# Attention and a gated MLP on one core: padding v, pairing the gate's left tokens, and moving the softmax reciprocals

## The chip, the cores and the metric

The kernel runs on one core of a Trainium2 chip. The core has five engines that work in parallel, each through its own queue in order: TensorE (PE in the profile, its weight loads PEld), VectorE (DVE), ScalarE (ACT), GpSimd (POOL) and SyncE (SP), which issues most DMAs. TensorE writes its results to PSUM, in banks of 512 fp32 numbers per partition. The metric is device time in microseconds; the profile is one further execution with its own time.

## The reference

For 8 batches and 12 heads of 448 tokens and 64 features:

```python
def _attn_ref(q, k, v, g_q, g_k):
    q_n, k_n = rmsnorm(q, g_q), rmsnorm(k, g_k)
    scores = matmul(q_n, k_n.T) / sqrt(64)
    attn = exp(scores - max(scores)); attn = attn / (sum(attn) + 1e-09)
    return matmul(attn, v)

def _moe_ref(x, w_in, g_ln, w_sg, b_sg, w_out):      # x: 448 x 768 per batch
    h = gelu(x @ w_in); u, v = h[..., :512], h[..., 512:]
    v_n = layernorm(v) * g_ln
    v_s = einsum('ts,bsd->btd', w_sg, v_n) + b_sg    # mixes tokens: the gate
    return x + (u * v_s) @ w_out
```

The attention result, heads side by side, is the MLP's x. Everything is in float32.

## The kernel before

**Numbers.** A factor in float32 is split into a high and a low float16 part, and a product is three matmuls: high x high, high x low, low x high. So most loops have three parts.

**Tokens.** 448 tokens are three and a half tiles of 128. The kernel holds them as seven chunks of 64 (`C7` = 7, `CM` = 3, `C4` = 4). Work goes by *pairs*: pair i is two heads, 48 pairs in all, six to a batch. Two pairs form a unit u, and their seven tiles of 128 query rows are run through together: tiles 0 to 2 belong to the first pair, tile 3 (`CM`) half to each, tiles 4 to 6 to the second.

**Scores** (L375 to L404). For each tile, matmuls of height 64 (one head in the upper 64 rows of the array, one in the lower) fill a PSUM tile of two banks; there are two such tiles (`NS` = 2). VectorE takes the row maxima (L392), ScalarE the exponentials with their sums (L394) and the copy to float16 (L397), VectorE the low part (L398), and a transposing DMA puts both into `at_all` (L403). After L398 the PSUM tile is free again.

**Reciprocals and row** (`recips`, L406 to L427). GpSimd adds 1e-9 to the sums (L413), VectorE inverts (L414), GpSimd makes high and low halves (L415, L416). Sixteen small matmuls spread the reciprocals along a row for each head (L423), and ScalarE copies it out of PSUM (L426). Row and pv use the same PSUM bank (`NV` = 1).

**pv** (L431 to L456). For each chunk and part, one matmul per head into the lower or upper 64 partitions of the result. Chunks 0 to 2 and 4 to 6 are full, 128 rows by 64 columns; chunk 3 has head 0 in the upper 64 partitions and head 1 in the lower, so its matmuls are quarters of the array, 64 x 64. Then VectorE multiplies by the row (L450), and high and low parts are made (L453, L454). v itself is loaded three pairs at a time (L286), squared for its scale (L353) and split (`vsplit`: L369 on ScalarE, L370 on VectorE). `vh` and `vl` have two buffers each.

**MLP** (`moe`, L477 to L655), one generator per batch: the half x @ w_in that becomes v (L499 to L521; the left 64 tokens first, as a half-width matmul pair at L513, then three tiles at L510), GELU, layer norm, the half that becomes u (L568), the gate (L589 to L609), and the output with the residual (L621 to L651). In the gate each of four blocks f of 128 features takes nine matmuls over the full token tiles and three over the 64 left tokens, which for f = 0, 1 lie in the upper 64 partitions and for f = 2, 3 in the lower. Then VectorE scales (L603), GpSimd multiplies by u (L604), ScalarE rounds (L605), GpSimd makes low parts (L607, L608). `gt` has two buffers; these products share three PSUM banks (`NM`).

**Order.** The work of one turn i is dealt out at L725 to L758: the score generator takes 8 or 6 steps, pv of the pair before `SV` = 4, the MLP of the batch before up to 11 from the third batch on (7 or 8 earlier), the weights 3. A generator's step ends at its next `yield`; the steps are dealt evenly over the turn. A batch's MLP has 46 or 50 steps, so at 11 a turn it fills a little over four of six turns. This order gives each instruction a priority (the MLP's is set 200 back); when the program is built, each engine's queue is ordered by these priorities among what a timeline model holds to be ready. On the chip each queue then runs strictly in that order.

Of the kernel before, what the change touches and what calls it, by code (L numbers as in the profile page):

```python
# [8 lines left out]
F32 = mybir.dt.float32  # L9
F32R = mybir.dt.float32r  # L10
F16 = mybir.dt.float16
BF16 = mybir.dt.bfloat16
I32 = mybir.dt.int32
AF = mybir.ActivationFunctionType
ALU = mybir.AluOpType
# [16 lines left out]

VC, UC = (3,), (0, 1)

SC, SV = 7, 4

NS, NV, NM = 2, 1, 3
NQK, NVR, RAWB = 2, 2, 3
NAT, NAH, NQT, NVH, HLB, GV = 3, 3, 2, 2, 3, 3
NOT, NX = 2, 12  # L40
# [6 lines left out]
def kernel(  # L47
# [16 lines left out]
    P = 128  # L64
# [217 lines left out]
        U[u] = dict(qk=qk)  # L282

    VR = {}

    def load_v(i):  # L286

        if i >= NI:  # L290
            return
        b, g = divmod(i, NP)
        vr = ld.tile([P, GV, C7, D], F32, name="vr", bufs=NVR)
        vp = vr.rearrange("p g c d -> p g (c d)")
        src = v[b, 2 * g:2 * (g + GV)].rearrange("(g h) (p c) d -> h p g (c d)", h=2, c=C7)
        for h, half, s0, c0, n in ((0, lo, 0, 0, C4), (0, hi, 0, C4, CM), (1, lo, C4, C4, CM), (1, hi, CM, 0, C4)):
            nc.sync.dma_start(out=vp[half, :, s0 * D:(s0 + n) * D], in_=src[h][:, :, c0 * D:(c0 + n) * D])
        for j in range(GV):
            VR[i + j] = vr[:, j].rearrange("p c d -> p (c d)")

# [42 lines left out]
    def vsquares(i):  # L343

        if i >= NI:
            return
        b, g = divmod(i, NP)
        if g == 0:
            VS["part", b] = sml.tile([P, NP // GV], F32, name="vpart", bufs=2)
        n = GV * C7 * D  # L350
        sk = prep.tile([P, n], BF16, name="sqv", tag="t4", bufs=HLB)
        x = VR[i]
        A.activation(out=sk, in_=bass.AP(tensor=x.tensor, offset=x.offset, ap=[list(x.ap[0]), [1, n]]), func=AF.Square,  # L353
                     accum_out=VS["part", b][:, g // GV:g // GV + 1])
# [8 lines left out]
    def vsplit(i):  # L363
        r = R.setdefault(i, {})
        sc = VS[i // NP]["sc"]
        vh, vl = (att.tile([P, C7, D], F16, name="v" + c, bufs=NVH) for c in "hl")
        vr = VR.pop(i)
        vf = vh.rearrange("p c d -> p (c d)")
        A.activation(out=vf, in_=vr, func=AF.Copy, scale=sc)  # L369
        V.scalar_tensor_tensor(out=vl.rearrange("p c d -> p (c d)"), in0=vr, scalar=sc, in1=vf, op0=ALU.mult, op1=ALU.subtract)  # L370
        r.update(vh=vh, vl=vl)

    at_all = att.tile([P, 2 * C7, NAT * S], F16, name="at", bufs=1)

    def scores(u):  # L375


        qt = U[u]["qt"]
        sums = sml.tile([P, C7, 2], F32, name="sums", bufs=2)
        U[u]["sums"] = sums  # L380
        for t in range(C7):
            ps = ps_s.tile([P, 2, 512], F32, name="s")

            rows = [(slice(0, P), t // C4)] if t != CM else [(lo, 0), (hi, 1)]
            for m, (qx, kx) in enumerate(((0, 2), (1, 2), (0, 3))):
                for h in range(2):
                    hs = slice(h * HP, (h + 1) * HP)
                    for r_, j in rows:
                        mm(out=ps[r_, h, 0:S], lhsT=qt[hs, qx, t * P + r_.start:t * P + r_.stop],  # L389
                           rhs=qt[hs, kx, j * S:(j + 1) * S], start=(m == 0), stop=(m == 2))  # L390
            nm = sml.tile([P, 2], F32, name="nm", bufs=6)
            V.tensor_reduce(out=nm, in_=ps[:, :, 0:S], axis=AX.X, op=ALU.max, negate=True)  # L392
            for h in range(2):
                A.activation(out=ps[:, h, 0:S], in_=ps[:, h, 0:S], func=AF.Exp, bias=nm[:, h:h + 1], accum_out=sums[:, t, h:h + 1])  # L394
            yield
            ahl = att.tile([P, 2, 2, S], F16, name="ahl", bufs=NAH)
            A.activation(out=ahl[:, 0], in_=ps[:, :, 0:S], func=AF.Copy)  # L397
            V.tensor_tensor(out=ahl[:, 1], in0=ps[:, :, 0:S], in1=ahl[:, 0], op=ALU.subtract)  # L398
            src = ahl.rearrange("p x h n -> p (x h n)")
            o = (NG * u * S + t * P) % (NAT * S)  # L400
            for r_ in ([slice(0, P)] if o + P <= NAT * S else [lo, hi]):
                o1 = (o + r_.start) % (NAT * S)
                nc.sync.dma_start_transpose(out=at_all[:, :, o1:o1 + r_.stop - r_.start], in_=src[r_])  # L403
            yield  # L404

    def recips(i):  # L406

        u, j = divmod(i, NG)
        cs = slice(0, C4) if j == 0 else slice(CM, C7)
        sums = U[u]["sums"][:, cs].rearrange("p t h -> p (t h)")  # L410
        x, y = (sml.tile([P, 2 * C4], F32, name=f"r{c}", bufs=2) for c in "xy")
        rh, rl = (sml.tile([P, 2 * C4], F16, name=f"r{c}", bufs=2) for c in "hl")
        G.tensor_scalar(out=x, in0=sums, scalar1=1e-9, scalar2=None, op0=ALU.add)  # L413
        V.reciprocal(out=y, in_=x)  # L414
        G.tensor_copy(out=rh, in_=y)  # L415
        G.tensor_tensor(out=rl, in0=y, in1=rh, op=ALU.subtract)  # L416
        ps = ps_v.tile([P, 512], F32, name="row", tag="pv")[:, 0:S]
        for n, t in enumerate(range(cs.start, cs.stop)):
            ks, o = (slice(0, P), t * P - j * S) if t != CM else ((lo, SM), (hi, 0))[j]
            for rx in (rh, rl):  # L420
                for h in range(2):
                    w = ks.stop - ks.start
                    mm(out=ps[h * HP:(h + 1) * HP, o:o + w], lhsT=rx[ks, 2 * n + h:2 * n + h + 1].broadcast_to([w, HP]),  # L423
                       rhs=ident_h[ks, ks], start=(n == 0 and rx is rh), stop=(n == CM and rx is rl), skip_group_check=True)
        row = att.tile([P, S], F32, name="row", bufs=1)
        A.activation(out=row, in_=ps, func=AF.Copy)  # L426
        return row  # L427

    XT = {}

    def pv(i):  # L431
        r = R[i]
        vh, vl = r["vh"], r["vl"]
        o = i % NAT * S

        steps = [[(slice(0, P), c + h * C4) if c < CM else (slice(h * HP, (h + 1) * HP), CM) for h in range(2)]
                 for c in range(C4)]
        blocks = [(vx, n, hx) for vx, n in ((vh, 0), (vl, 0), (vh, C7)) for hx in steps]

        blocks = blocks[CM::C4] + [x for n, x in enumerate(blocks) if n % C4 != CM]  # L440
        row = recips(i)
        yield
        ps = ps_v.tile([P, 512], F32, name="pv")[:, 0:S]
        for k_, (vx, n, hx) in enumerate(blocks):
            for h, (ks, c) in enumerate(hx):
                mm(out=ps[h * HP:(h + 1) * HP], lhsT=vx[ks, c], rhs=at_all[ks, n + c, o:o + S],  # L446
                   start=(k_ == 0), stop=(k_ == len(blocks) - 1), skip_group_check=True)
            if k_ in (4, 8):
                yield
        V.tensor_tensor(out=ps, in0=ps, in1=row, op=ALU.mult)  # L450
        xh = xp.tile([P, S], F16, name="xh")
        xl = xp.tile([P, S], F16, name="xl")
# [1 line left out]
        V.tensor_tensor(out=xl, in0=ps, in1=xh, op=ALU.subtract)  # L454
        XT[i] = (xh, xl)
        del R[i]  # L456


    def cluster(acts, done):
# [17 lines left out]
    def moe(b, early=False):  # L477
# [21 lines left out]
        for st, (t, g) in enumerate(steps):  # L499
# [17 lines left out]
                psv[t] = vg[:, tiles[t][1]]  # L517
            if early and t == 1 and g == NP - 1:
                cluster([gelu_v(i) for i in range(2)], done)
            if st % 2 == 1:  # L520
                yield  # L521
        cluster([gelu_v(t) for t in order if not early or t == CM or t > 1], done)
        for t in range(CK):
# [54 lines left out]
                 for f in range(FT)], done)  # L578
        yield
        gh = mlp.tile([P, FT, S], F32R, name="gh", tag="vggh")  # L580
        gl = []
        vh, vl = V2["vh"], V2["vl"]
        half = slice(b % 2 * HP, (b % 2 + 1) * HP)
        if b % 2 == 0:
# [1 line left out]
        else:  # L586
            gth, gtl, _ = GT[b - 1]
        bb = W["bb"]
        for f in range(FT):  # L589
            ps = ps_m.tile([P, 512], F32, name="ms_", tag="mm")  # L590
            n = 0
            for t in range(CK):
                p0, p1, o = 0, P, t * DH + f * P
                if t == CM:
                    p0 = f // 2 * HP
                    p1, o = p0 + HP, t * DH + f % 2 * P
                for vx, wx in ((vh, ws_h), (vh, ws_l), (vl, ws_h)):
                    mm(out=ps[:, 0:S], lhsT=vx[p0:p1, o:o + P], rhs=wx[p0:p1, t], start=(n == 0), stop=(n == 11))
                    n += 1
                if t == 1:  # L600
                    yield
            gt = mlp.tile([P, S], F32, name="gt", tag="gt", bufs=NOT)
            V.scalar_tensor_tensor(out=gt, in0=ps[:, 0:S], scalar=W["gw"][:, f:f + 1], in1=bb, op0=ALU.mult, op1=ALU.add)  # L603
            G.tensor_tensor(out=gt, in0=gt, in1=u[f], op=ALU.mult)  # L604
            A.activation(out=gh[:, f], in_=gt, func=AF.Copy)  # L605
            gl.append(mlp.tile([P, S], F32R, name="gl", tag="ug", bufs=5))
            G.tensor_tensor(out=gl[f], in0=gt, in1=gh[:, f].bitcast(F32), op=ALU.subtract)  # L607
            G.tensor_tensor(out=gtl[:, f, half], in0=gt[:, SM:S], in1=gh[:, f, SM:S].bitcast(F32), op=ALU.subtract)  # L608
            yield  # L609
        idn = VS[b]["idn"]  # L610
        om = [out[x].rearrange("(p c) e -> c p e", c=C7) for x in (b - b % 2, b)]
# [180 lines left out]
```

## Time and profile before

| | |
|---|---|
| median of three runs | 1035.32 us (1034.66 to 1037.95) |
| profiled execution | 1033.44 us, its span 1031.6 us |
| mean granted TensorE clock | 0.916 of full speed |
| 0 to 100 us | TensorE busy 28.4 us, VectorE 76.2, ScalarE 61.1 |
| 600 to 700 us | TensorE busy 92.8 us, VectorE 76.7, ScalarE 80.2 |

"Busy" is the share in which at least one instruction of the engine runs. In tables of waits, each line names the waiting engine and line, what ended the wait, and then the total, the count and the longest in us. In lines that group instructions, after the shapes and the count (x48) stand busy us and mean ns of one, then the idle time before them and what ended it. A shape such as 64*128 on a matmul is rows by columns of the array that it uses.

### The profile page before, as it was taken

The page shows a single profiled execution, that of the slowest core. Times are in us where ns is not written, and L with a number is a line of the kernel's source. Part 1 is how long each engine was busy: PE and PEld are TensorE (multiplying, and loading weights), DVE is VectorE, ACT ScalarE, POOL GpSimd, SP SyncE. Part 2 cuts the span into 40 slices and gives each one's busy share as a digit, 9 for nine tenths or more (in the row PEclk, how much of TensorE's full clock was granted, in tenths as well). Part 3 has the DMA queues.
Part 4 walks back from the last instruction along what each step waited for, and adds up shares of the span by engine and source line. Part 5 has one row for each costly group of instructions (what it writes and reads, how often), then busy time and mean ns, then how long its engine had stood idle before and what let it go on. Part 6 is the DMA issues. An engine that isn't in the chain of part 4 may idle for free.

```text
span 1031.6 us, 16639 instructions
## 1 busy us (share of the span) xinstructions
PE 829.0 (80%) x5844; PEld 421.1 (41%) x5844; DVE 733.3 (71%) x1332; ACT 738.1 (72%) x1449; POOL 386.9 (38%) x403
## 2 busy tenths in 40 slices
PE   0243666858798997899689998999779998998798
PEld 0111222324444563346234553446324563454246
DVE  6698888999587667786677758786669666766230
ACT  3767779877868767777768767987777776877351
POOL 1468614567253505243251606341533414030021
PEclk9976687969899999999699998999889999999899
DMA  6998748776886398478886488959967676556102
GB/s 163 214 228 191 166 115 196 185 176 130 181 197 150 88 204 180 98 170 145 186 175 147 99 194 183 182 123 176 194 142 160 141 166 125 106 135 123 40 1 62
DMA packets 448004, 155.70 MB, mean 151 GB/s; under 512 B 404336, under 2 KB 441776, under 8 KB 447920
## 3 DMA queue, kind: packets, MB, share of 16 engines
q1 hardware_dynamic: 447344, 154.18, 69.0%
q8 instruction: 46, 0.75, 0.3%
q10 hardware_dynamic: 576, 0.46, 0.2%
q14 instruction: 38, 0.31, 0.1%
HBM read 43.57 MB, written 11.01 MB: 53 GB/s over the span
## 4 chain that ended last, share of the span: by engine, by line
PE 34%; DVE 21%; ACT 19%; DMA 11%; issue 8%; SPq 4%; POOL 4%; ACTq 0%; POOLq 0%; DVEq 0%
PE pv L446 6%; ACT s L394 5%; DVE ahl L398 5%; PE s L389 4%; DVE nm L392 3%; ACT ahl L397 2%; DMA vr<-in_v_dram 2%; ACT sqk L308 2%; DMA raw<-in_moe_w_in_dram 2%; DMA at<-ahl 2%; POOL qk L330 2%; DMA qt<-hl 2%; DMA qk<-in_k_dram 2%; ACT hl L334 2%; SPq L336 1%
## 5 line engine op out<-in xcount | busy, mean ns | idle before, releaser
L394 ACT ACTIVATE s<-s,nm 128x448 f32<-128x448 f32 x336 | 204.0, 607 | 109.8 <-DVE nm L392 106.8
L398 DVE TENSOR_TENSOR ahl<-s,ahl 128x896 f16<-128x896 f32 x168 | 182.1, 1085 | 100.8 <-ACT ahl L397 99.8
L389 PE MATMUL s<-qt 64*128 64x448 f16 (+1 forms) x1152 | 143.2, 390 | 110.7 <-DVE ahl L398 76.4
L392 DVE TENSOR_REDUCE nm<-s 128x2 f32<-128x896 f32 x168 | 180.8, 1082 | 40.5 <-PE s L389 40.0
L397 ACT ACTIVATE ahl<-s 128x896 f16<-128x896 f32 x168 | 153.4, 920 | 5.3 <-DMA at<-ahl 3.1
L446 PE MATMUL pv<-at,vh 128*64 128x448 f16 (+1 forms) x768 | 122.7, 398 | 16.4 <-DMA at<-ahl 7.6
L413 POOL TENSOR_SCALAR rx<-sums 128x8 f32<-128x8 f32 x48 | 13.4, 278 | 311.8 <-ACT s L394 310.4
L389 PEld LDWEIGHTS <-qt 64*128 64x128 f16 (+1 forms) x1152 | 45.3, 102 | 177.2 <-issue 135.9
L330 POOL TENSOR_TENSOR qk<-qk,ny 128x896 f32<-128x896 f32 x46 | 80.8, 1774 | 85.8 <-DVE ny L125 82.3
L335 POOL TENSOR_TENSOR hl<-qk,hl 128x896 f16<-128x896 f32 x46 | 87.7, 1917 | 55.1 <-ACT hl L334 54.5
L568 PEld LDWEIGHTS <-wi 128*128 128x128 f16 x576 | 55.9, 100 | 60.2 <-issue 14.1
L446 PEld LDWEIGHTS <-vh 128*64 128x64 f16 (+1 forms) x768 | 43.4, 117 | 84.3 <-issue 70.2
L309 DVE TENSOR_REDUCE ss<-sqk 128x14 f32<-128x896 f32 x48 | 51.8, 1080 | 29.2 <-ACT sqk L308 28.9
L394 ACT ACTIVATION_READ_ACCUMULATOR s<-s,nm 128x1 f32 x336 | 67.7, 201 | 0.0
L329 POOL TENSOR_TENSOR qk<-qk,gg 128x896 f32<-128x896 f32 x23 | 48.0, 2085 | 43.2 <-ACT sqk L308 39.3
L423 PE MATMUL row<-ident_h,rh 128*64 128x128 f16 (+1 forms) x384 | 36.7, 240 | 31.7 <-POOL rh L415 24.0
L604 POOL TENSOR_TENSOR gt<-gt,u 128x448 f32<-128x448 f32 x32 | 38.5, 1206 | 60.1 <-DVE gt L603 55.9
L446 PE MATMUL pv<-at,vl 128*64 128x448 f16 (+1 forms) x384 | 60.4, 394 | 0.0
L334 ACT ACTIVATE hl<-qk 128x896 f16<-128x896 f32 x48 | 44.9, 947 | 15.9 <-POOL qk L330 8.4
L308 ACT ACTIVATE sqk<-qk 128x896 f32<-128x896 f32 x48 | 45.6, 951 | 8.2 <-DVE ss L309 4.4
L510 PEld LDWEIGHTS <-xh 128*128 128x128 f16 x288 | 27.0, 101 | 49.2 <-issue 21.9
L369 ACT ACTIVATE vh<-vr,v_s 128x448 f16<-128x448 f32 x48 | 31.9, 668 | 19.7 <-PE pv L446 19.6
(996 smaller groups left out, 1960.8 us busy)
## 6 DMA issues: line engine op xcount, KB each, us to landing
out_dram<-ot SPq DMA_DIRECT2D x56, 192.0 KB, 2.9
vr<-in_v_dram SPq DMA_DIRECT2D x32, 192.0 KB, 3.3
raw<-in_moe_w_in_dram SPq DMA_DIRECT2D x12, 512.0 KB, 5.7
qk<-in_q_dram SPq DMA_DIRECT2D x47, 128.0 KB, 2.8
qk<-in_k_dram SPq DMA_DIRECT2D x47, 128.0 KB, 2.8
vr<-in_v_dram SPq DMA_DIRECT2D x32, 144.0 KB, 3.3
qk<-in_q_dram SPq DMA_DIRECT2D x47, 96.0 KB, 2.6
qk<-in_k_dram SPq DMA_DIRECT2D x47, 96.0 KB, 2.6
```

Of the source, the lines that this page charges most:

```text
L308: A.activation(out=skv, in_=U[u]["qk"][:, x].rearrange("p h c d -> p (h c) d"), func=AF.Square)
L309: V.tensor_reduce(out=SS[u][:, x], in_=skv, axis=AX.X, op=ALU.add)
L330: E.tensor_tensor(out=qk, in0=qk, in1=r["rs"][:, x * SSW:(x + 1) * SSW].unsqueeze(2).broadcast_to([P, SSW, D]), op=ALU.mult)
L334: A.activation(out=h_, in_=r["qk"][:, x], func=AF.Copy)
L335: E.tensor_tensor(out=l_, in0=r["qk"][:, x], in1=h_, op=ALU.subtract)
L389: mm(out=ps[r_, h, 0:S], lhsT=qt[hs, qx, t * P + r_.start:t * P + r_.stop], rhs=qt[hs, kx, j * S:(j + 1) * S], start=(m == 0), stop=(m == 2))
L392: V.tensor_reduce(out=nm, in_=ps[:, :, 0:S], axis=AX.X, op=ALU.max, negate=True)
L394: A.activation(out=ps[:, h, 0:S], in_=ps[:, h, 0:S], func=AF.Exp, bias=nm[:, h:h + 1], accum_out=sums[:, t, h:h + 1])
L397: A.activation(out=ahl[:, 0], in_=ps[:, :, 0:S], func=AF.Copy)
L398: V.tensor_tensor(out=ahl[:, 1], in0=ps[:, :, 0:S], in1=ahl[:, 0], op=ALU.subtract)
L446: mm(out=ps[h * HP:(h + 1) * HP], lhsT=vx[ks, c], rhs=at_all[ks, n + c, o:o + S], start=(k_ == 0), stop=(k_ == len(blocks) - 1), skip_grou ...
L568: done = mm(out=ps[:, 0:S], lhsT=ww[:, g, f * P:(f + 1) * P], rhs=xx, start=(n == 0), stop=(n == 17))
```

## The change

Four things are done.

- **v is padded.** Two fixed buffers hold v with eight chunks; chunk 3 has head 0 in the upper 64 partitions and zeros below, chunk 4 zeros above and head 1 below. The zeros are written once at the start. Both chunks together are one 128 x 128 factor, so the shared chunk takes three full matmuls for six quarter ones.
- **pv is one block.** Its first step does nothing, the second does row, all matmuls and the result, the third ends it; `SV` is 3 for 4. 
- **The reciprocals** are made right behind the last scores of each pair (tile 3 and tile 6), all four operations on VectorE; `recip_row` keeps the small matmuls.
- **The gate** takes f in pairs (0, 2) and (1, 3): nine matmuls each, a break after each, then the left tokens alternating between the two, then both results. In the MLP's first product the breaks inside the left-token tile go (the first and the last batch, which run in the `early` form, keep them).

```diff
-SC, SV = 7, 4
+SC, SV = 7, 3
...
+    C8 = C7 + 1
+    vr_all = [ld.tile([P, GV, C8, D], F32, name=f"vr{n}", bufs=1) for n in range(NVR)]
+    for x in vr_all:
+        G.memset(x[hi, :, CM], 0.0)
+        G.memset(x[lo, :, C4], 0.0)
...
-        for h, half, s0, c0, n in ((0, lo, 0, 0, C4), (0, hi, 0, C4, CM), (1, lo, C4, C4, CM), (1, hi, CM, 0, C4)):
+        for h, half, s0, c0, n in ((0, lo, 0, 0, C4), (0, hi, 0, C4, CM), (1, lo, C4 + 1, C4, CM), (1, hi, C4, 0, C4)):
...
+    def recips(i):
+        u, j = divmod(i, NG)
+        cs = slice(0, C4) if j == 0 else slice(CM, C7)
+        sums = U[u]["sums"][:, cs].rearrange("p t h -> p (t h)")
...
+        U[u]["r", j] = rh, rl = [sml.tile([P, 2 * C4], F16, name=f"r{c}", bufs=3) for c in "hl"]
+        V.tensor_scalar(out=x, in0=sums, scalar1=1e-9, scalar2=None, op0=ALU.add)
+        V.reciprocal(out=y, in_=x)
+        V.tensor_copy(out=rh, in_=y)
+        V.tensor_tensor(out=rl, in0=y, in1=rh, op=ALU.subtract)
...
+            if t in (CM, C7 - 1):
+                recips(NG * u + (t > CM))
             yield
...
-        row = recips(i)
         yield
+        row = recip_row(i)
         ps = ps_v.tile([P, 512], F32, name="pv")[:, 0:S]
-        for k_, (vx, n, hx) in enumerate(blocks):
-            for h, (ks, c) in enumerate(hx):
-                mm(out=ps[h * HP:(h + 1) * HP], lhsT=vx[ks, c], rhs=at_all[ks, n + c, o:o + S],
-                   start=(k_ == 0), stop=(k_ == len(blocks) - 1), skip_group_check=True)
-            if k_ in (4, 8):
-                yield
+        parts = ((vh, 0), (vl, 0), (vh, C7))
+        for k_, (vx, n) in enumerate(parts):
+            mm(out=ps, lhsT=vx[:, CM:CM + 2].rearrange("p c d -> p (c d)"), rhs=at_all[:, n + CM, o:o + S],
+               start=(k_ == 0), stop=False, skip_group_check=True)
+        for c in range(CM):
+            for vx, n in parts:
+                for h in range(2):
+                    mm(out=ps[h * HP:(h + 1) * HP], lhsT=vx[:, c + h * (C4 + 1)], rhs=at_all[:, n + c + h * C4, o:o + S],
+                       start=False, stop=(c == CM - 1 and n == C7), skip_group_check=True)
...
-            if st % 2 == 1:
+            if st % 2 == 1 and (early or t != CM or g == NP - 1):
                 yield
...
+        for f0 in range(2):
+            psf = {f: ps_m.tile([P, 512], F32, name="ms_", tag="mm") for f in (f0, f0 + 2)}
+            for f, ps in psf.items():
+                n = 0
+                for t in range(CM):
+                    o = t * DH + f * P
+                    for vx, wx in ((vh, ws_h), (vh, ws_l), (vl, ws_h)):
+                        mm(out=ps[:, 0:S], lhsT=vx[:, o:o + P], rhs=wx[:, t], start=(n == 0), stop=False)
+                        n += 1
+                yield
+            for n, (vx, wx) in enumerate(((vh, ws_h), (vh, ws_l), (vl, ws_h))):
+                for f, ps in psf.items():
+                    p0, o = f // 2 * HP, CM * DH + f0 * P
+                    mm(out=ps[:, 0:S], lhsT=vx[p0:p0 + HP, o:o + P], rhs=wx[p0:p0 + HP, CM], start=False, stop=(n == 2))
+            for f, ps in psf.items():
+                gt = mlp.tile([P, S], F32, name="gt", tag="gt", bufs=NOT)
...
```

`vsquares` and `vsplit` take eight chunks for seven, so their operations are 512 wide for 448 (1536 for 1344 in the squares).

More of the change, by code (lines that the diff above doesn't have):

```diff
@@ L292, in load_v @@
         b, g = divmod(i, NP)
-        vr = ld.tile([P, GV, C7, D], F32, name="vr", bufs=NVR)
+        vr = vr_all[i // GV % NVR]
         vp = vr.rearrange("p g c d -> p g (c d)")
         src = v[b, 2 * g:2 * (g + GV)].rearrange("(g h) (p c) d -> h p g (c d)", h=2, c=C7)
-        for h, half, s0, c0, n in ((0, lo, 0, 0, C4), (0, hi, 0, C4, CM), (1, lo, C4, C4, CM), (1, hi, CM, 0, C4)):
+        for h, half, s0, c0, n in ((0, lo, 0, 0, C4), (0, hi, 0, C4, CM), (1, lo, C4 + 1, C4, CM), (1, hi, C4, 0, C4)):
             nc.sync.dma_start(out=vp[half, :, s0 * D:(s0 + n) * D], in_=src[h][:, :, c0 * D:(c0 + n) * D])
@@ L349, in vsquares @@
             VS["part", b] = sml.tile([P, NP // GV], F32, name="vpart", bufs=2)
-        n = GV * C7 * D
+        n = GV * C8 * D
         sk = prep.tile([P, n], BF16, name="sqv", tag="t4", bufs=HLB)
@@ L365, in vsplit @@
         sc = VS[i // NP]["sc"]
-        vh, vl = (att.tile([P, C7, D], F16, name="v" + c, bufs=NVH) for c in "hl")
+        vh, vl = (att.tile([P, C8, D], F16, name="v" + c, bufs=NVH) for c in "hl")
         vr = VR.pop(i)
@@ L373, with recip_row @@
     at_all = att.tile([P, 2 * C7, NAT * S], F16, name="at", bufs=1)
+    def recips(i):
+        u, j = divmod(i, NG)
+        cs = slice(0, C4) if j == 0 else slice(CM, C7)
+        sums = U[u]["sums"][:, cs].rearrange("p t h -> p (t h)")
+        x, y = (sml.tile([P, 2 * C4], F32, name=f"r{c}", bufs=2) for c in "xy")
+        U[u]["r", j] = rh, rl = [sml.tile([P, 2 * C4], F16, name=f"r{c}", bufs=3) for c in "hl"]
[3 more added lines that the diff above has]
+        V.tensor_tensor(out=rl, in0=y, in1=rh, op=ALU.subtract)
+    def recip_row(i):
+        u, j = divmod(i, NG)
+        cs = slice(0, C4) if j == 0 else slice(CM, C7)
+        rh, rl = U[u]["r", j]
+        ps = ps_v.tile([P, 512], F32, name="row", tag="pv")[:, 0:S]
+        for n, t in enumerate(range(cs.start, cs.stop)):
+            ks, o = (slice(0, P), t * P - j * S) if t != CM else ((lo, SM), (hi, 0))[j]
+            for rx in (rh, rl):
+                for h in range(2):
+                    w = ks.stop - ks.start
+                    mm(out=ps[h * HP:(h + 1) * HP, o:o + w], lhsT=rx[ks, 2 * n + h:2 * n + h + 1].broadcast_to([w, HP]),
+                       rhs=ident_h[ks, ks], start=(n == 0 and rx is rh), stop=(n == CM and rx is rl), skip_group_check=True)
+        row = att.tile([P, S], F32, name="row", bufs=1)
+        A.activation(out=row, in_=ps, func=AF.Copy)
+        return row
     def scores(u):
@@ L403, in scores @@
                 nc.sync.dma_start_transpose(out=at_all[:, :, o1:o1 + r_.stop - r_.start], in_=src[r_])
+            if t in (CM, C7 - 1):
+                recips(NG * u + (t > CM))
             yield
[L406 to L427, printed above, removed]
     XT = {}
@@ L434, in pv @@
         o = i % NAT * S
[L436 to L440, printed above, removed]
-        row = recips(i)
         yield
+        row = recip_row(i)
         ps = ps_v.tile([P, 512], F32, name="pv")[:, 0:S]
-        for k_, (vx, n, hx) in enumerate(blocks):
-            for h, (ks, c) in enumerate(hx):
-                mm(out=ps[h * HP:(h + 1) * HP], lhsT=vx[ks, c], rhs=at_all[ks, n + c, o:o + S],
-                   start=(k_ == 0), stop=(k_ == len(blocks) - 1), skip_group_check=True)
-            if k_ in (4, 8):
-                yield
+        parts = ((vh, 0), (vl, 0), (vh, C7))
[4 more added lines that the diff above has]
+            for vx, n in parts:
+                for h in range(2):
+                    mm(out=ps[h * HP:(h + 1) * HP], lhsT=vx[:, c + h * (C4 + 1)], rhs=at_all[:, n + c + h * C4, o:o + S],
+                       start=False, stop=(c == CM - 1 and n == C7), skip_group_check=True)
         V.tensor_tensor(out=ps, in0=ps, in1=row, op=ALU.mult)
@@ L580, in moe @@
         gh = mlp.tile([P, FT, S], F32R, name="gh", tag="vggh")
-        gl = []
+        gl = {}
         vh, vl = V2["vh"], V2["vl"]
@@ L588, in moe @@
         bb = W["bb"]
[L589 to L608, printed above, removed]
@@ new lines, in moe @@
+        for f0 in range(2):
[7 more added lines that the diff above has]
+                        n += 1
+                yield
+            for n, (vx, wx) in enumerate(((vh, ws_h), (vh, ws_l), (vl, ws_h))):
[4 more added lines that the diff above has]
+                gt = mlp.tile([P, S], F32, name="gt", tag="gt", bufs=NOT)
+                V.scalar_tensor_tensor(out=gt, in0=ps[:, 0:S], scalar=W["gw"][:, f:f + 1], in1=bb, op0=ALU.mult, op1=ALU.add)
+                G.tensor_tensor(out=gt, in0=gt, in1=u[f], op=ALU.mult)
+                A.activation(out=gh[:, f], in_=gt, func=AF.Copy)
+                gl[f] = mlp.tile([P, S], F32R, name="gl", tag="ug", bufs=5)
+                G.tensor_tensor(out=gl[f], in0=gt, in1=gh[:, f].bitcast(F32), op=ALU.subtract)
+                G.tensor_tensor(out=gtl[:, f, half], in0=gt[:, SM:S], in1=gh[:, f, SM:S].bitcast(F32), op=ALU.subtract)
```

## Prediction

> **What bounds the kernel now.** I read the page's first lines first, then a table of busy time by stretches.
>
> ```profile
> span 1031.6 us, 16639 instructions
> PE 829.0 (80%) x5844; PEld 421.1 (41%) x5844; DVE 733.3 (71%) x1332; ACT 738.1 (72%) x1449; POOL 386.9 (38%) x403
> ```
>
> ```profile
> core 0: us, PE busy (x) PEld busy (x) DVE busy (x) ACT busy (x) POOL busy (x), PEclk, DMA share, GB/s
> 58.00:180.00 122.00, 66.47 (x434) 27.34 (x434) 106.97 (x180) 94.36 (x191) 66.02 (x54) 0.70 0.78 174
> 180.00:300.00 120.00, 94.30 (x664) 47.94 (x663) 103.30 (x189) 92.00 (x177) 64.64 (x60) 0.86 0.76 172
> ...
> 300.00:900.00 600.00, 541.85 (x3908) 276.36 (x3905) 434.39 (x817) 454.52 (x901) 211.86 (x231) 0.95 0.73 155
> ...
> 420.00:540.00 120.00, 103.95 (x730) 52.28 (x727) 83.90 (x151) 89.12 (x178) 42.60 (x46) 0.91 0.73 150
> ...
> 780.00:900.00 120.00, 115.08 (x845) 59.85 (x844) 86.25 (x173) 89.40 (x181) 34.52 (x43) 1.00 0.66 139
> ...
> 970.00:1032.00 62.00, 53.58 (x312) 32.98 (x308) 13.01 (x37) 22.32 (x34) 10.04 (x12) 0.99 0.10 26
> ```
>
> No engine is full over the whole span, so each stage has its own limit. From 58 to 300 us, while weights are still being prepared, VectorE is the busiest (107 of 122 us, then 103 of 120). From 300 to 900 us it is TensorE, 542 of 600 us or 90%, against 72% and 76% for VectorE and ScalarE. After 970 us only the last batch's MLP is left, and TensorE is again nearly full. So TensorE work or TensorE waits that go after 300 us shorten the run by most of their length, and VectorE work added before 300 us lengthens it. Then the waits, first of the whole run, the last line of 250 to 970 us alone (in total, times, longest):
>
> ```profile
> POOL rx L413 <- ACT s L394: 310.4, 31, 21.5
> ACT s L394 <- DVE nm L392: 106.8, 58, 6.0
> ...
> PE s L389 <- DVE ahl L398: 76.4, 35, 9.0
> PEld L446 <- issue: 75.7, 189, 3.4
> ...
> PE row L423 <- POOL rh L415: 24.0, 13, 5.3
> ...
> ACT vh L369 <- PE pv L446: 19.6, 12, 3.3
> ...
> DVE ry L414 <- POOL rx L413: 15.5, 19, 1.9
> ...
> DVE gt L603 <- POOL gtl L608: 5.3, 5, 2.4
> ...
> PE pv L446 <- ACT row L426: 3.6, 5, 1.4
> ```
>
> ```profile
> PE row L423 <- POOL rh L415: 16.5, 9, 5.3
> ```
>
> The largest wait of TensorE is for a score buffer that VectorE must release; the change does not touch it. The next is the one it aims at: 24.0 us in 13 stops, in which the row matmuls stand at the head of TensorE's queue until GpSimd has made the reciprocal's halves. GpSimd's own 310.4 us at L413 cost nothing by themselves, but they hold up whatever is queued behind them.
>
> **The gate's left tokens.** The timeline of TensorE in one gate (start, duration, instruction):
>
> ```profile
> 563.96 0.74 PE L389 MATMUL s<-qt 64*128 64x448 f16 x6
> 564.63 0.36 PE L598 MATMUL ms__6148<-ws_h,vl 128*128 128x448 f16 x1
> ...
> 565.70 0.35 PE L598 MATMUL ms__6183<-ws_h,vh 128*128 128x448 f16 x1
> 565.89 0.35 PE L598 MATMUL ms__6183<-ws_l,vh 128*128 128x448 f16 x1
> ...
> 567.21 0.35 PE L598 MATMUL ms__6183<-ws_h,vl 128*128 128x448 f16 x1
> 567.50 0.36 PE L598 MATMUL ms__6183<-ws_h,vh 64*128 64x448 f16 x1
> ...
> 567.88 0.35 PE L598 MATMUL ms__6183<-ws_h,vl 64*128 64x448 f16 x1
> 568.16 0.36 PE L598 MATMUL ms__6222<-ws_h,vh 128*128 128x448 f16 x1
> ```
>
> Matmuls are pipelined, so the distance between starts is the price: 0.19 us for 448 columns (565.70 to 565.89). Into and out of the half-height shape it is 0.29 and 0.28 us (567.21 to 567.50, 567.88 to 568.16), so a change of shape costs 0.10 and 0.09. One f takes 568.16 - 565.70 = 2.46 us, two take 4.92. The six half-height score matmuls, which alternate between the upper and lower rows, take 564.63 - 563.96 = 0.67 us: three passes of 0.19 and one change of shape. So two half-height matmuls in different rows share a pass. A pair of f's in the new order needs 18 full passes and 3 shared ones, 21 x 0.19 = 3.99, and two changes, 0.19: 4.18 us, 0.74 less. There are 2 pairs in each of 8 batches: 16 x 0.74 = 11.8 us of TensorE, at 90% 10.7 (bounds 0 and 11.8). Against it: the pair's two results are evicted together, so GpSimd's work on them bunches.
>
> ```profile
> L604 POOL TENSOR_TENSOR gt<-gt,u 128x448 f32<-128x448 f32 x32 | 38.5, 1206 | 60.1 <-DVE gt L603 55.9 <-ACT u L577 2.1 <-ACT s L394 2.0
> L607 POOL TENSOR_TENSOR gl<-gt,gh 128x448 fp32r<-128x448 f32 x32 | 36.8, 1150 | 7.9 <-ACT gh L605 7.8
> ```
>
> Per f that is 1.21 + 1.15 us and a small slice, some 2.5; a pair takes GpSimd 5 us where TensorE needs 4.2 for the next. With two gt buffers the second pair's evictions on VectorE can wait for GpSimd, and score reductions are queued behind them. The wait is there already at 5.3 us; I add 1, at worst another 10.6. In the last batch the output matmuls follow at once, and f = 1 now comes out of GpSimd third; I add 1 us, which takes back most of that batch's 1.5.
>
> **Reciprocals to VectorE.** The row matmuls' wait goes: 24.0 us at most. The 7.5 before 250 us lie where TensorE has slack; the 16.5 after it count in full: -16.5 (bounds 0, if the stop only moves to the next score buffer, and -24.0). VectorE pays for it.
>
> ```profile
> L414 DVE RECIPROCAL ry<-rx 128x8 f32<-128x8 f32 x48 | 9.4, 196 | 15.8 <-POOL rx L413 15.5
> ...
> L370 DVE SCALAR_TENSOR_TENSOR vl<-vr,v_s,vh 128x448 f16<-128x448 f32 x48 | 36.6, 764 | 3.0 <-ACT vh L369 3.0
> ```
>
> ```profile
> 985.12 0.16 DVE L119 TENSOR_TENSOR lt<-lx,ly 128x4 f32<-128x4 f32 x1
> 985.32 0.16 DVE L120 TENSOR_TENSOR lt<-lt,ly 128x4 f32<-128x4 f32 x1
> ```
>
> ```profile
> L369 ACT ACTIVATE vh<-vr,v_s 128x448 f16<-128x448 f32 x48 | 31.9, 668 | 19.7 <-PE pv L446 19.6
> L426 ACT ACTIVATE row<-row 128x448 f32<-128x448 f32 x48 | 26.0, 542 | 6.5 <-PE row L423 6.3
> ```
>
> Tiny dependent operations follow each other at 0.20 us (985.12 to 985.32). Three more in 48 pairs are 29 us; the 15.5 us of standing for GpSimd's sum go; net 13.3. They wait for nothing new: the sums are written by the exponentials, ahead of the copy for which the subtraction before them has waited. What they delay is the next score reduction, by 0.8 us twice in seven tiles, and ScalarE behind it. The zero-padded chunk makes vl and vh 512 wide for 448: a seventh more, 5.2 us of VectorE and 4.6 of ScalarE, and a little for the squares. Together 18.5 us on VectorE; I count a quarter in full, as a quarter of the span (58 to 300 us) is VectorE's, and a quarter of the rest: +8 (bounds 0 and +18.5). GpSimd loses three operations and its place behind the sums; I count no gain for that. The memsets of the padding stand at the start, where GpSimd has nothing to do yet: nothing. The loads move the same bytes.
>
> **pv in one block.**
>
> ```profile
> 548.18 0.38 PE L446 MATMUL pv<-at,vh 64*64 64x448 f16 x2
> 548.39 0.35 PE L446 MATMUL pv<-at,vl 64*64 64x448 f16 x2
> ...
> 573.34 0.85 PE L446 MATMUL pv<-at,vh 64*64 64x448 f16 x6
> 574.12 0.74 PE L389 MATMUL s<-qt 64*128 64x448 f16 x6
> 574.79 0.38 PE L446 MATMUL pv<-at,vh 128*64 128x448 f16 x2
> ```
>
> Two quarter-size matmuls already share a pass of 0.2 us (548.18 to 548.39). Three padded full-size ones take the same three passes, and a change of shape to the half-width ones remains. So the padding itself saves nothing (bounds -5 and +5, one change of shape per pair either way). What can be saved are interruptions, as by the scores at 574.12: two changes of shape, 0.2 us. The weight loads of pv stood idle for no visible reason 189 times; two such breaks per pair, 96, must stay, so at most 93 x 0.1 = 9 us go. I take 4, and 1 more for the left-token tile of the MLP's first product, now without breaks: -5 (bounds 0 and -10). The blocks are finished at half of a turn where they ended at seven eighths, so vh comes free sooner: ScalarE's 19.6 us for it shrink. ScalarE is not the bound: -3 (bounds 0 and -10).
>
> One thing gets worse. The row and pv share one PSUM bank, and the pv matmuls may start only when ScalarE has copied the row out, 0.54 us. Before, a quarter of a turn of other work lay between the two; now they are neighbours by priority. The 3.6 us of this wait will grow: +6, a quarter of 48 x 0.54 (bounds 0 and +50, with a copy of about 0.5 us still ahead of it on ScalarE each time). The cover is other TensorE work that is ready, mostly the MLP of the batch before.
>
> **Sum** against the profiled execution's 1033.4: -10.7 + 1 + 1 - 16.5 + 8 - 5 - 3 + 6 = -19.2, so 1014.2. That is the span and 1.8 us around it, and lies 1.9 below the median of the three runs, 1035.3; so I forecast 1016.
>
> **The rivals.** First, slower: *the row's copy becomes the stop of every pair.* My sum has 3.6 + 6 = 9.6 us for this wait. If it is 1 us in each of 48 pairs, the time is 1016 + 48 - 9.6 = 1054. The gain is gone when the wait reaches 9.6 + 19 = 29 us, 0.6 us per pair, which is hardly more than the bare copy. For it: one bank, and ScalarE at 76%, in order. Against it: TensorE stood for the row only 5 times, and there is MLP work in four of six turns. Chance 0.18.
>
> Second, no change: *what TensorE saves comes back as waits for VectorE and ScalarE.* ScalarE's 106.8 us for the maxima and TensorE's 76.4 for score buffers show a chain that runs through VectorE, which gets 18.5 us more. If the bound after 300 us is this chain, the gate's 10.7 us fall away and the row's wait gives half: 1016 + 10.7 + 8.3 = 1035. Against it: 90% for TensorE. Chance 0.15.
>
> Third, better: *the clock rises.* The granted clock is 0.91 in 420 to 540 us with TensorE busy 104 us, and 1.00 in 780 to 900 with 115. Stops of up to 5.3 us go. If the mean of 300 to 900 rises from 0.95 to 0.98, the 542 us of TensorE shrink by 3%, 16 us more: 1000. Chance 0.17. [...]
>
> That the change does not do what it says is possible for the block: program order is only a priority, and scores may still come between. That costs the 5 us, not the sign.
>
> **Numbers.** Forecast 0.50 at 1016. Range 996 to 1044: it takes in the third case and half of the first. A difference under 0.3%, 3 us, cannot be told from none. Faster by more: forecast and third case, 0.67, and 0.03 of the second: 0.70. Same: 0.07 of the second and 0.03 of the first: 0.10. Slower: 0.15 of the first and 0.05 of the second: 0.20.
>
> **What would show it.** In the profile after: no wait of TensorE for GpSimd's rh, and 24 us less there; two f's of the gate in 4.2 us, six half-height matmuls in 0.67; VectorE busier by 30 to 35 us; TensorE's wait for the row's copy under 10 us. I am wrong if that wait is above 25 us, or if TensorE's wait for VectorE's subtraction grows by as much as the row's wait falls.

## The result and the profile after

The change made the kernel slower: 1064.8 us (1062.75 to 1066.75, 4 runs) against 1036.3 for the kernel before (1034.66 to 1037.95), a ratio of 1.0275 with a 95% interval of 1.0243 to 1.0307. The profiled execution's span is 1065.0 us against 1031.6. The page's first lines after, and the stretches of before again (columns as there: length, then busy us and instructions of TensorE, its weight loads, VectorE, ScalarE, GpSimd, then the clock):

```profile
span 1065.0 us, 16265 instructions
PE 832.9 (78%) x5700; PEld 421.0 (40%) x5700; DVE 780.2 (73%) x1476; ACT 748.0 (70%) x1449; POOL 355.2 (33%) x263
```

```profile
58.00:180.00 122.00, 60.87 (x414) 25.13 (x411) 107.21 (x193) 91.69 (x182) 59.80 (x39) 0.74 0.75 170
180.00:300.00 120.00, 91.95 (x566) 45.27 (x567) 103.21 (x187) 87.01 (x166) 54.54 (x39) 0.82 0.72 155
300.00:900.00 600.00, 520.75 (x3668) 265.34 (x3670) 453.39 (x876) 446.19 (x871) 198.62 (x139) 0.93 0.72 153
```

VectorE is 46.9 us busier (780.2 for 733.3), where I had put 30 to 35. From 300 to 900 us TensorE fell from 542 to 521 of 600 us, as a kernel looks that waits more: the stretch now holds 3668 matmuls, 3908 before. VectorE rose from 434 to 453, and the granted clock is 0.93 there for 0.95. The waits (total, count, longest), first the ones I had expected to go, shrink or grow:

```profile
ACT s L428 <- DVE nm L426: 102.6, 57, 5.7
PE s L423 <- DVE ahl L432: 70.3, 41, 8.4
DVE pv L460 <- PE pv L458: 39.8, 20, 7.4
ACT vh L374 <- PE pv L458: 35.1, 18, 4.5
PE row L403 <- DVE rh L389: 23.3, 10, 8.3
DVE rx L387 <- ACT s L428: 16.5, 18, 2.7
```

TensorE's wait for GpSimd's rh (24.0 us) has not gone, it has another owner: 23.3 us for VectorE's rh. VectorE's wait for GpSimd (15.5) has become one for the last exponential's sum (16.5). VectorE's wait for pv nearly doubled from 22.0, ScalarE's for vh's buffer from 19.6. The stops for the row's copy, my first rival, did not come: the row tile's own list of waiters has them at 4.5 us in 3 (3.6 before), of which the table of waits puts 1.8 us down to ScalarE's copy:

```profile
  PE pv L453: 4.5, 3
```

Neither of the two signs of being wrong that I had named appeared: this wait stayed far below 25 us, and TensorE's wait for VectorE's subtraction fell from 76.4 to 70.3. The time rose all the same, so the loss came by a way that I had not listed.

And the gate. TensorE's timeline shows the pair ms__6031 and ms__6032 one after the other; the first block's left tokens are done before the second block's first matmul:

```profile
582.55 0.35 PE L607 MATMUL ms__6031<-ws_h,vl 128*128 128x448 f16 x1
582.83 0.36 PE L614 MATMUL ms__6031<-ws_h,vh 64*128 64x448 f16 x1
...
583.22 0.35 PE L614 MATMUL ms__6031<-ws_h,vl 64*128 64x448 f16 x1
...
585.28 0.35 PE L607 MATMUL ms__6032<-ws_h,vh 128*128 128x448 f16 x1 [0.51 <-DVE gt L617]
...
587.46 0.35 PE L614 MATMUL ms__6032<-ws_h,vl 64*128 64x448 f16 x1
```

Of the 96 half-height matmuls of the gate none stands next to one of the other block of its pair. The second block waited for VectorE to empty a PSUM bank (the 0.51 us at 585.28). Probably the builder's timeline model saw that wait coming and put the left tokens that were ready ahead of it; that this is its reason was not tried. What the diff writes is a priority, not an order.

### The profile page after: what moved, and what is told of

Read it like the earlier page. It is cut to its first block, busy times and chain, and to the rows that moved or that the text cites. A ratio compares the mean times of both kernels' runs of the same rounds, so it can differ in the third digit from the quotient of the medians.

```text
span 1065.0 us, 16265 instructions
## 1 busy us (share of the span) xinstructions
PE 832.9 (78%) x5700; PEld 421.0 (40%) x5700; DVE 780.2 (73%) x1476; ACT 748.0 (70%) x1449; POOL 355.2 (33%) x263
## 4 chain that ended last, share of the span: by engine, by line
DVE 31%; PE 30%; ACT 13%; DMA 11%; issue 8%; SPq 3%; POOL 3%; ACTq 0%; DVEq 0%; POOLq 0%
DVE ahl L432 5%; DVE nm L426 5%; PE pv L458 4%; ACT s L428 4%; DMA vr<-in_v_dram 3%; ACT ahl L431 3%; PE s L423 3%; DVE vl L375 2%; DMA qt<-hl 2%; DVE ss L314 2%; DMA at<-ahl 2%; PE pv L453 2%; DMA raw<-in_moe_w_in_dram 1%; SPq L302 1%; POOL qk L335 1%
## 5 line engine op out<-in xcount | busy, mean ns | idle before, releaser
L423 PE MATMUL s<-qt 64*128 64x448 f16 (+1 forms) x1152 | 142.0, 388 | 98.5 <-DVE ahl L432 70.3
L458 PE MATMUL pv<-at,vh 128*64 128x448 f16 x576 | 100.8, 406 | 0.0
L453 PE MATMUL pv<-at,vh 128*128 128x448 f16 x96 | 40.2, 418 | 38.3 <-DMA at<-ahl 19.8
L460 DVE TENSOR_TENSOR pv<-pv,row 128x448 f32<-128x448 f32 x48 | 30.1, 627 | 44.7 <-PE pv L458 39.8
L374 ACT ACTIVATE vh<-vr,v_s 128x512 f16<-128x512 f32 x48 | 34.5, 722 | 35.2 <-PE pv L458 35.1
L458 PE MATMUL pv<-at,vl 128*64 128x448 f16 x288 | 58.2, 402 | 0.0
L403 PE MATMUL row<-ident_h,rh 128*64 128x128 f16 (+1 forms) x384 | 37.0, 239 | 25.8 <-DVE rh L389 23.3
L458 PEld LDWEIGHTS <-vh 128*64 128x64 f16 x576 | 36.4, 124 | 48.7 <-issue 35.1
```

The costliest lines, as they stand in the source:

```text
L453: mm(out=ps, lhsT=vx[:, CM:CM + 2].rearrange("p c d -> p (c d)"), rhs=at_all[:, n + CM, o:o + S], start=(k_ == 0), stop=False, skip_group_ ...
L458: mm(out=ps[h * HP:(h + 1) * HP], lhsT=vx[:, c + h * (C4 + 1)], rhs=at_all[:, n + c + h * C4, o:o + S], start=False, stop=(c == CM - 1 and ...
```

## The experiments

Three theories to begin with: **A**, the reciprocals on VectorE cost the time; **B**, pv's block does; **C**, no part has a price of its own, each edit re-deals the order of the queues. Names with b_ are the kernel before with something added, with a_ the changed kernel with something undone, with c_ pairs of parts. Ratios are to the kernel before, with 95% intervals.

**The parts alone.** b_pad has the padding, with the old steps:

> The kernel before with the padding alone: v in eight chunks, three full matmuls for six quarter ones in pv, everything else as before. Theory A (the reciprocals on VectorE cost the time: their conversions last while GpSimd holds something that VectorE needs, and VectorE is 50 us busier): 1036 to 1042, as 5 to 7 us of VectorE and 5 of ScalarE are added. Theory B (pv in one block and half a turn later costs the time): the same. Theory C (no single part, every edit re-deals the order of the queues): anywhere from 1025 to 1050.

b_block has this, with the old quarter-size matmuls. It also moves the reciprocals, which are still GpSimd's here, and the row from the first step to the second:

```diff
-SC, SV = 7, 4
+SC, SV = 7, 3
-        row = recips(i)
         yield
+        row = recips(i)
...
-            if k_ in (4, 8):
-                yield
...
         del R[i]
+        yield
```

> The kernel before with pv as one block alone: first step empty, then reciprocals on GpSimd, row, all matmuls and the result in the second of three steps. Theory A: 1036, within 5. Theory B: 1050 or more, with ScalarE's wait for pv at vh up from 20 us to 35 and VectorE's wait for pv up from 22 to 40, as in the changed kernel. Theory C: 1025 to 1050.

b_rec has the change's `recips` behind the scores, the row where it was; b_gate the two MLP edits:

> The kernel before with the reciprocals alone: all four operations on VectorE right behind tile 3 and tile 6 of the scores, the row in its old place. Theory A: 1055 to 1065, VectorE 40 to 50 us busier, the conversion to the high half with single operations of 1.5 us. Theory B: 1036 or faster, since the row's wait of 24 us for GpSimd goes. Theory C: 1025 to 1050.

> The kernel before with the MLP's two edits alone: the gate's blocks in pairs as written, and no breaks in the left-token tile. In the changed kernel none of the 96 half-height matmuls of the gate stands next to one of the other block of its pair, so I expect no shared pass here either. Theories A and B: 1036, within 5. Theory C: 1025 to 1050.

| run | median us | ratio |
|---|---|---|
| b_pad | 1035.4 | 0.9992 (0.9970 to 1.0014) |
| b_block | 1051.2 | 1.0138 (1.0094 to 1.0182) |
| b_rec | 1045.0 | 1.0084 (1.0054 to 1.0114) |
| b_gate | 1030.2 | 0.9938 (0.9913 to 0.9962) |

So the reciprocals (A) and the block (B) each have a part, A's smaller than it said. C is not ruled out: its range of 1025 to 1050 holds three of the four, and misses b_block by 1 us, while b_gate lies 1 us outside what A and B gave it. The product of the four is 1.015; 1.2% belong to the parts together. b_gate is faster than either kernel; here 21 of the 96 half-height matmuls stand behind one of the other block, where its expectation had none, and the changes of shape on TensorE fall from 763 to 643.

**Parts undone, and two parts in another form.** a_blk puts pv's steps back, a_pool the three small operations on GpSimd (`V.` to `G.` at the addition, the conversion and the difference):

> The changed kernel with pv's steps put back: row in the first of four steps, the padded matmuls in three parts (5, 4 and 3 blocks of them), the rest of the change kept. The parts alone gave ratios of 0.999 (padding), 1.014 (block), 1.008 (reciprocals), 0.994 (MLP edits); their product, 1.015, leaves 1.2% of the 2.75% to the parts together. Theory B (the block costs most, alone and by what it does to the others): 1037, the product of the other three. Theory A (VectorE): 1050, as only the block's own 1.4% goes.

> The changed kernel with the addition, both conversions and the difference on GpSimd again, but at their new place behind the last scores; only the inversion on VectorE. Theory A (VectorE's 50 us of small operations and its standing while GpSimd works): 1050 or less. Theory B: 1060 to 1065, as the block is still there.

b_gatef ties the pair, b_late moves the block to the last step:

```diff
+            with tc.issue_after(full.ins):
                 for n, (vx, wx) in enumerate(((vh, ws_h), (vh, ws_l), (vl, ws_h))):
...
         row = recips(i)
         yield
+        yield
+        yield
...
-            if k_ in (4, 8):
-                yield
```

> The kernel before with the gate in pairs, where the left tokens of both blocks are bound to come behind the pair's last full matmul, so that the two blocks' matmuls do alternate. Without that tie (the run of the MLP edits) the time was 1030 and no two alternated. If two half-height matmuls share a pass as my prediction had it, 48 passes of 0.19 us and half the changes of shape go: 10 us less than that run where TensorE is the bound, 1020 to 1025; 1030 to 1036 if TensorE's saving only becomes a wait for the two results that now end together.

> The kernel before with pv's matmuls in one block, but dealt at the last of four steps with the result, the row at the first as before. Theory B1 (unbroken block: the scores behind it come late, whatever its place): 1045 to 1055, as with the block at half of the turn. Theory B2 (the place: the result is due at half of a turn, and VectorE stands for it with the maxima behind): 1036, within 5, and VectorE's wait for pv back near 22 us from 50.

| run | median us | ratio |
|---|---|---|
| a_blk | 1067.7 | 1.0294 (1.0258 to 1.0330) |
| a_pool | 1063.8 | 1.0247 (1.0197 to 1.0297) |
| b_gatef | 1036.1 | 1.0002 (0.9978 to 1.0027) |
| b_late | 1042.2 | 1.0057 (1.0041 to 1.0073) |

a_blk met neither expectation: the block costs 14 us alone, and taking it out of the whole gives nothing back. a_pool came where B had put it. It takes 41.9 us off VectorE's busy time (780.2 to 738.3) and no clear time off the kernel, so VectorE's busy time by itself is not what is paid for. It does not separate the theories even so: the inversion stays on VectorE, and there it stands 19.6 us for GpSimd's sum in place of 16.5 for ScalarE's. b_late lies between its two theories, 1.0057 against b_block's 1.0138; VectorE's wait for pv, 50.3 us with the block at half of a turn, is 15.9 at the end. Since b_late also has the reciprocals and the row back in the first step, the 0.8% between the two belong to these places together. b_gatef is the sharpest. Its expectation says that without the tie no two alternated; it was 21. In its timeline two half-height matmuls start together:

```profile
584.92 0.35 PE L596 MATMUL ms__6149<-ws_h,vl 128*128 128x448 f16 x1
585.21 0.36 PE L604 MATMUL ms__6148<-ws_h,vh 64*128 64x448 f16 x1
585.21 0.36 PE L604 MATMUL ms__6149<-ws_h,vh 64*128 64x448 f16 x1
...
585.60 0.35 PE L604 MATMUL ms__6148<-ws_h,vl 64*128 64x448 f16 x1
585.60 0.35 PE L604 MATMUL ms__6149<-ws_h,vl 64*128 64x448 f16 x1
585.88 0.36 PE L596 MATMUL ms__6211<-ws_h,vh 128*128 128x448 f16 x1
```

From the pair's first matmul at 581.70 to the next pair's at 585.88 are 4.18 us, the figure that I had worked out. TensorE's busy time in the whole run shows most of the saving (829.0 us before, for as many matmuls), and the time does not:

```profile
PE 820.6 (79%) x5844; PEld 423.2 (41%) x5844; DVE 737.5 (71%) x1332; ACT 738.6 (71%) x1449; POOL 387.0 (37%) x403
```

TensorE's wait for score buffers is 89.6 us here, 76.4 before: a longer wait for VectorE stands beside the saving, as the second half of the expectation had it.

**Four repeats that were meant to test C.** Each has one number changed, `MOFF` 190 or 210 for 200:

> The kernel before with one number changed that has nothing to do with the change: the MLP's priority offset 190 for 200. Same instructions, another order of the queues. Theory C (the order alone moves the time by per cents): more than 5 us away from 1036, either way. Theories A and B, by which single parts have their price: 1036, within 5.

> The same with 210. Theory C: more than 5 us away from 1036. Theories A and B: 1036, within 5.

> The changed kernel with the offset 190. Theory C: more than 5 us away from 1064, and if the loss is an accident of one order, nearer to 1040. Theories A and B: 1064, within 5.

> The changed kernel with the offset 210. Theory C: more than 5 us away from 1064. Theories A and B: 1064, within 5.

Measured: 1037.0, 1035.0, 1065.8 and 1067.4 us, ratios 1.0001, 0.9984, 1.0275 and 1.0272. But the offset did not do what the expectation says: the queues of TensorE, VectorE and ScalarE came out the same row for row. So the four show only how well a time repeats (0.2%), and theory C stands untested by them. In every other run the queues of all three differ from those of both kernels, also where nothing was edited.

**Pairs of parts, one edit alone, and one tie.**

> The kernel before with the reciprocals on VectorE and the MLP edits, without padding and block. Alone they gave 1045 and 1030, a product of 1039. Theory D (the MLP edits' gain needs an order that the other parts spoil: fewer changes of shape, 643 for 763): if the reciprocals spoil it, 1050 or more and changes of shape back near 700; if not, 1039.

> The kernel before with the padding and the MLP edits. Alone they gave 1035 and 1030, a product of 1030. Theory D: if the padding spoils the MLP edits' gain, 1036 or more and changes of shape back near 700; if not, 1030.

> The kernel before with one edit alone: no breaks in the left-token tile of the MLP's first product. The MLP edits together gave 1030 and took the changes of shape inside that product from 104 to 50; the gate in tied pairs without this edit gave 1036 although a pair took the 4.18 us of my prediction. If the gain is this edit's: 1030, with about 50 such changes. If it is the untied gate's: 1036.

b_rect is b_rec and this:

```diff
-            V.tensor_tensor(out=ahl[:, 1], in0=ps[:, :, 0:S], in1=ahl[:, 0], op=ALU.subtract)
+            sub = V.tensor_tensor(out=ahl[:, 1], in0=ps[:, :, 0:S], in1=ahl[:, 0], op=ALU.subtract)
...
             if t in (CM, C7 - 1):
-                recips(NG * u + (t > CM))
+                with tc.issue_after(sub.ins):
+                    recips(NG * u + (t > CM))
```

> The run of the reciprocals alone, 1045, with one tie more: VectorE takes them behind the subtraction of the tile, not ahead of it. There VectorE stood 17.0 us in 20 stops for the last exponential's sum. If that standing is what the part costs, 1036 to 1039; if it is the operations themselves, 40 us with those that last while GpSimd works, 1045.

| run | median us | ratio | product of its parts |
|---|---|---|---|
| c_recgate | 1048.5 | 1.0141 (1.0101 to 1.0181) | 1.002 |
| c_padgate | 1051.7 | 1.0167 (1.0149 to 1.0184) | 0.993 |
| b_cm | 1036.6 | 1.0006 (0.9987 to 1.0025) | |
| b_rect | 1037.3 | 1.0013 (0.9993 to 1.0032) | |

Theory D, which the first of these expectations states, fits c_recgate, which is slow and has 677 changes of shape, 83 of them inside the first product. It fails in c_padgate: there those inside the first product stayed at 49 and all changes of shape fell to 615, fewer than in b_gate. TensorE had as little to do as in b_gate (812.0 us busy for 811.6), and the kernel was still 1.67% slower than before, where b_gate is 0.62% faster:

```profile
PE 812.0 (78%) x5700; PEld 419.6 (40%) x5700; DVE 733.0 (70%) x1332; ACT 746.8 (71%) x1449; POOL 386.4 (37%) x407
```

This is the nearest that the runs come to theory C. Against it stand b_pad, b_cm, b_gatef and b_rect: each has queues in another order than before, and each takes the time of before within 0.13%.

b_cm halves those changes of shape (51 for 104) and gains nothing. b_rect gives nearly all of the reciprocals' 0.84% back, and its four operations are as slow as ever (below), so it was not their length that was paid for:

```profile
L382 DVE TENSOR_SCALAR rx<-sums 128x8 f32<-128x8 f32 x48 | 19.9, 414 | 0.0
...
L384 DVE CAST rh<-ry 128x8 f16<-128x8 f32 x48 | 17.8, 370 | 1.0
L385 DVE TENSOR_TENSOR rl<-ry,rh 128x8 f16<-128x8 f32 x48 | 14.0, 291 | 1.0
L383 DVE RECIPROCAL ry<-rx 128x8 f32<-128x8 f32 x48 | 9.5, 198 | 0.9
```

**The same two questions in the whole.** a_tie is the changed kernel with that tie, a_mlp the changed kernel without the MLP edits:

> The changed kernel with the tie of the run before: VectorE takes the reciprocals behind the tile's subtraction. Alone the tie took 8 us off the reciprocals' part. If VectorE's standing for the sums (16.5 us in 18 stops in the changed kernel) costs the same here: 1055 to 1058. If the whole has another bound, which hides it: 1064.

> The changed kernel without the MLP's two edits: padding, block and reciprocals as changed. The MLP edits gained 6 us alone, but with the padding the two together gave 1052 and with the reciprocals 1048. If the MLP edits turn the other parts to a loss: 1045 or less. If the parts' own prices hold: the product of the other three, 1.021, 1058. If the MLP edits still gain in the whole: 1070.

a_tie: 1050.7 us, ratio 1.0140 (1.0105 to 1.0175), below the range expected. One tie takes 14 of the 29 us back, more than the 8 it gave alone. a_mlp: 1057.4 us, 1.0242 (1.0184 to 1.0300): within its interval the product of the three other parts, 1.021, so in the whole the MLP edits' 0.6% is no longer there.

## Why the prediction was wrong

**"They wait for nothing new."** This step failed, and two runs with one tie each (b_rect, a_tie) put a price on it. I argued from the code, in which the reciprocals stand behind the subtraction. The builder put them ahead of it in all 48 pairs, in b_rec too; the sums are ready before ScalarE's copy is (below, the addition starts at 555.99, when the copy has only begun). The changed kernel's timeline of VectorE, ScalarE and GpSimd at tile 3 of one unit:

```profile
555.99 0.92 ACT L431 ACTIVATE ahl<-s 128x896 f16<-128x896 f32 x1
555.99 0.40 DVE L387 TENSOR_SCALAR rx<-sums 128x8 f32<-128x8 f32 x1 [0.28 <-ACT s L428]
556.42 0.20 DVE L388 RECIPROCAL ry<-rx 128x8 f32<-128x8 f32 x1
556.66 1.37 DVE L389 CAST rh<-ry 128x8 f16<-128x8 f32 x1
...
557.97 1.88 POOL L340 TENSOR_TENSOR hl<-qk,hl 128x896 f16<-128x896 f32 x1
558.07 1.80 DVE L390 TENSOR_TENSOR rl<-ry,rh 128x8 f16<-128x8 f32 x1
...
559.79 1.08 DVE L432 TENSOR_TENSOR ahl<-s,ahl 128x896 f16<-128x896 f32 x1
```

The copy ends at 555.99 + 0.92 = 556.91; the subtraction starts at 559.79, 2.9 us later, behind four operations on eight columns. This tile is one of the longer cases: over the 48 tiles with reciprocals the mean from the copy's end to the subtraction's start is 0.91 us, against 0.45 before and 0.48 in a_tie.

Where does the delay reach TensorE? Not at the score buffers that the subtraction frees: that wait is 70.3 us in the changed kernel and 81.7 in a_tie. It is seen one step further on, in pv's wait for the transposing DMA that follows the subtraction (before, changed, a_tie):

```profile
PE pv L446 <- DMA at<-ahl: 7.6, 3, 3.0
PE pv L453 <- DMA at<-ahl: 19.8, 9, 2.9
PE pv L454 <- DMA at<-ahl: 2.9, 2, 2.2
```

In b_rec it is 12.8 us, in b_rect 2.1. These differences are near the 14 and 8 us that the ties gave back. But the tie re-dealt the rest of the queues as well, and no run moved this wait alone, so that the time went this way is likely and not shown.

**The price of a small operation.** I took 0.20 us each from a stretch in which GpSimd stood still (0.00 us busy from 984.7 to 986.4 us). Where GpSimd works, some of them last until its operation ends (minimum, median, maximum in ns):

```profile
L388 DVE RECIPROCAL ry<-rx x48: 186/203/205, 45.9 to 992.9; 128x8 f32<-128x8 f32 x48
L389 DVE CAST rh<-ry x48: 154/172/1648, 46.1 to 993.1; 128x8 f16<-128x8 f32 x48
L390 DVE TENSOR_TENSOR rl<-ry,rh x48: 154/167/1803, 49.3 to 994.2; 128x8 f16<-128x8 f32 x48
```

The median is mine, the mean is not: 400 ns for the conversion and 376 for the difference. rl above ran from 558.07 to 559.87, GpSimd's operation from 557.97 to 559.85; the reciprocal never exceeds 205 ns. Of the 144 additions, conversions and differences 23 lasted over 0.4 us, and each of these ended within 0.06 us of a GpSimd operation's end. Theory A's words, that GpSimd holds something that VectorE needs, fit these rows; what that would be no row shows, and that GpSimd's work is the cause was not tried. By b_rect the length alone costs little: the four operations take 61 us there, and the kernel is at 1.0013.

**-16.5 us for the row.** Failed: 23.3 us of the 24.0 are still there, in VectorE's name; with the tie it is 12.9 in a_tie. An operation that is dealt earlier is not early on the chip when it stands in a queue that runs late.

**-10.7 us for the gate.** Two things failed. The pairs were not built, which I had held possible for pv's block alone and not for the gate. And with the pairs built and the 4.18 us met, b_gatef gained nothing. So the larger error lies in the first part: TensorE's busy time, 90% from 300 to 900 us, was not what sets the time. c_padgate and b_gate have the same 812 us of it and lie 2% apart. My second rival said that what TensorE saves comes back as waits in a chain through the score buffers. b_gatef fits that (89.6 us of that wait for 76.4); the whole change does not (70.3), and the rival gave 1035, with no loss in it.

**-5 and -3 us for pv in one block.** The sign was wrong: alone it costs 14 us. I counted changes of shape and vh's buffer, and left out VectorE, which stands for pv's product with the maxima of the next scores queued behind it (before, b_block, b_late):

```profile
DVE pv L450 <- PE pv L446: 22.0, 11, 7.7
DVE pv L448 <- PE pv L446: 50.3, 21, 7.0
DVE pv L450 <- PE pv L448: 15.9, 7, 7.9
```

With the row and the reciprocals back in the first step and the result in the last (b_late) more than half of the cost goes, and this wait with it. vh's wait rose where I had it shrink, from 19.6 to 35.1 us, and to 22.5 in b_block alone. The left-token tile failed too: in the changed kernel the changes of shape inside the MLP's first product rose from 104 to 131 although its breaks were gone.

**The padding at 0** and the loads were right (0.9992), though in c_padgate the padding was not free. For the row's copy +6 was too high, it is +1 at most, and the first rival fell. That VectorE's load counts most at the start is not refuted: VectorE's product of the thirteenth pair starts 23 us later than before (340 us for 317), that of the nineteenth 17, and the span grew by 33. So half or more of the loss arises early. VectorE was no busier there, though: 107.2 us of 122 and 103.2 of 120, as before.

**The third rival's clock** went the other way. The granted clock from 300 to 900 us is 0.93 for 0.95. By that rival's own arithmetic, 2% of 542 us, some 11 us of the loss could be this. It may as well be a consequence of the waits; that stops lower the clock was the rival's guess, which no run tries, and none holds the clock fixed. With TensorE busy 100.4 of 120 us from 420 to 540 us and 103.2 from 780 to 900, the changed kernel has 0.94 in both stretches. Alone it does not order the kernels: b_gate is the fastest with a mean clock of 0.908 in its runs, and the kernel before has 0.914.

**What stays open.** Half of the loss, 14 us, goes when VectorE takes the reciprocals behind the subtraction (a_tie). The other half has the size of the block's own price, but a_blk did not give it back, and padding with MLP edits cost 1.67% in c_padgate though neither does alone. pv's wait for the DMA cannot be the whole either: a_pool has 7.6 us of it, as before, and is no faster. All these runs, the tied ones too, have another order of the queues, which no run could hold fixed, so theory C is open for every price here, and I can name no cause for the second half.

The fastest kernel here is b_gate, the kernel before with the MLP edits: 1030.2 us, 0.9938. Its gain is not explained either: neither the left-token tile alone (b_cm) nor the tied pairs alone have it, and the untied gate alone was not run.

## What to carry to other kernels

A busy engine is not yet the bound: TensorE lost 8.4 of its 829.0 busy us in b_gatef and no time went. Before counting what an edit saves, ask which instruction stands directly behind the moved one in the in-order queue, and who waits for that; where a scheduler deals the queues, read the order that it built, since source order is only a wish. A tie of one instruction behind another is a cheap experiment, and here it was worth half the loss.

## What the runs showed of the hardware

In the changed kernel an eight-column VectorE conversion or difference lasted 0.17 us at the median and up to 1.65 and 1.80 us while GpSimd worked; the reciprocal of the same size stayed within 186 to 205 ns. Two half-height matmuls in different rows of the array, into different PSUM tiles, started within 0.01 us of each other, and the next two 0.20 us behind them (b_gatef, at 585.21 and 585.41).
